# Order of the first transfers and placing of the tail's weights in a decode block with cached attention

## The chip, the cores and the metric

The kernel runs on one core of a Trainium2 chip. The metric is the device time of one execution in microseconds (us). Three runs of the kernel before gave 1055.89, 1056.32 and 1057.12 us, so the median is 1056.32 us. The profile is of one further execution.

## The reference

One token passes through an attention block and a feed-forward block, each scaled and shifted by "modulations" that are computed from a condition vector `c` of 640 numbers:

```python
mod = (silu(c) @ w_mod)                   # 6 vectors of 640: sa, ca, ga, sb, cb, gb
h = layernorm(x) * (1 + ca) + sa          # x: 640 numbers
q = h @ wq                                # 32 heads of 192
o = softmax(q @ k_cache.T * 192**-0.5) @ v_cache     # per head, 8192 cached positions
x = x + ga * (o @ wo)
h = layernorm(x) * (1 + cb) + sb
x = x + gb * (relu(h @ w1 + b1)**2 @ w2 + b2)        # 640 -> 1536 -> 640
```

Everything is in 32-bit floats. The two caches hold 32 heads x 8192 positions x 192 numbers each, which is 6144 KB per head and cache; they make up nearly all of what is read.

## The kernel before

**Tiles.** The positions of a head lie 64 to each of the 128 partitions. There are two buffers for keys, `k_t[0]` and `k_t[1]`, and two for values, `v_t[0]` and `v_t[1]`; head h uses number h mod 2 of each. A transfer of keys also carries, behind the keys, a weight block: with even heads the query weights of the next pair of heads, with odd heads the output weights of an earlier pair (7104 KB in all). Heads 1 and 30 carry none. The names below number the heads from 0 and write k2 for the keys of head 2, v1 for the values of head 1.

**The start.** The first transfer, `wm0`, brings the weights of the first two modulations and the first query weights into `v_t[1]`. Then come k0 in two halves, k1 and v0. While they arrive, the first layernorm and the first query are computed (lines 157 to 206); `m_wm0` (line 207) marks the end of the last reader of `wm0`, after which `v_t[1]` is free for v1.

**A head.** VectorE (DVE in the profile) multiplies the keys by the query in place, in two halves (L288), and sums over each row (L293, L297), with GpSimd (POOL) folding part of it (L291). L301 takes the largest score of a partition, a matmul (L231) brings the partitions together, L306 takes the maximum and ScalarE (ACT) the exponentials (L312). TensorE (PE) multiplies them with the values in 24 matmuls of 512 columns (L225, `pe_values`). With each even head TensorE also computes the query of the next pair out of the weights that lie behind that head's keys in `k_t[0]` (L237, `pe_query`, five matmuls of 384 columns). After a pair, VectorE normalises the two outputs (`dve_project`, L328 to L333), a small matmul turns them (L242), and GpSimd multiplies them with the output weights in `k_t[1]` (L319, L322, `pool_project`).

**The order of the work.** No scheduler sets it: each engine runs its instructions as the code writes them. TensorE's order is that of `pe_pair`: values of the last pair's second head, maximum of the even head, query of the next pair, turn of the last pair, values of the even head, maximum of the odd head, sums. Pairs 1 to 14 run in a hardware loop on TensorE (L267 on); pair 15 is written out behind it, without a query.

**The queue of transfers.** SyncE (SP) issues all transfers from one queue, in the order of the code, and waits there until a buffer is free. In the loop over heads (line 344 on), the transfer of k(h+2) stands first: it waits for the end of VectorE's and GpSimd's work on k(h), with an even h also for the query that is read from the same buffer (`done["q", i + 1]`), with an odd h for the output projection. The transfer of v(h+1) stands behind it and waits for the values matmuls of head h-1, or with head 0 for `m_wm0`.

**The tail.** The last four kinds of transfer bring weights into buffers that have come free: `wm1` (output weights of the last pair and the modulations ga, sb, cb) into `k_t[0]`, `w1` into `v_t[0]`, and `gw2` (the modulation weights of the last gate, gb, and then `w2`) into `k_t[1]` in four pieces, the first with the gate's 1600 KB and the first six of w2's twelve blocks. TensorE computes ga (20 matmuls of 160 columns, L158), the last turn (L427), the attention output (L435), sb and cb in three portions between the steps of the second layernorm (L158 again, 320 columns), `h @ w1` (L461), the gate gb (L158, from the first piece of `gw2`) and the product with w2 (L485, 48 matmuls of 160 columns, waiting for the pieces one by one). VectorE adds and squares between them (L467 to L470) and finishes with L488 and L489.

The semaphore of a transfer is in the last argument of `dma`: `w_sem[1]` for `wm1`, `w_sem[2]` for `w1`, `w_sem[3]` to `w_sem[6]` for the four pieces.

Of the kernel before, what the change touches and what calls it, by code (L numbers as in the profile page):

```python
# [35 lines left out]
SMALL = 2 * KB + FB + KB  # L36
W0 = KB * 2 * D + WQ + SMALL
W1M = WO + KB * 3 * D
GW2 = KB * D + FB * D
W2_CUT = (KB * D + 6 * D, KB * D + 9 * D, KB * D + 11 * D, GW2)  # L40
EPS = 1e-5


# [23 lines left out]
        return self.sem, self.n  # L67


def block_kernel(nc, kw, ky, vc, wm0, wm1, w1, gw2, out):  # L70
# [37 lines left out]
    def dma(dst, src, s):  # L108
        nc.sync.dma_start(dst, src).then_inc(s, 16)
# [3 lines left out]
    def keys_of(h):  # L113
        return kw[WITH_W.index(h)] if h in WITH_W else ky[WITHOUT_W.index(h)]
# [38 lines left out]
    def mod(target, w, n, blocks):  # L153

        for b in blocks:
            wb = w[:, b * n * D:(b + 1) * n * D].rearrange("p (m n) -> p m n", m=n)
            for g in range(G):
                i = pe.matmul(target[32 * g:32 * (g + 1), :n * DG], e_t[:, b:b + 1].to_broadcast([P, 32]),  # L158
                              wb[:, :, DG * g:DG * (g + 1)], start=(b == 0), stop=(b == KB - 1))
        return T.mark(i)  # L160
# [57 lines left out]
    def pe_values(s):  # L218
        T.take(b_sem[s], 16)
        T.take(tk_p[s])  # L220
        t = v_t[s][:, :].rearrange("p (j g n) -> p j g n", g=NV, n=E * ED)
        n = NPOS // E
        for j in range(n):
            for g in range(NV):
                i = pe.matmul(ps_o[s][32 * g:32 * (g + 1), :], p_t[s][:, E * j:E * (j + 1)].rearrange("p e r -> p (e r)"),  # L225
                              t[:, j, g], start=(j == 0), stop=(j == n - 1))
# [42 lines left out]
    for i in range(2, NPAIR - 1):  # L269
        pe_pair(i, False)  # L270
    pe_pair(NPAIR - 1, True)


    landed = {s: [0, 0] for s in range(2)}
# [1 line left out]
    def dve_keys(h, between):  # L276
        s = h % 2
        q = qb[h // 2 % 2][:, DH * (h % 2):DH * (h % 2 + 1)]
        t = k_t[s][:, :HD].rearrange("p (i d) -> p i d", d=DH)
        V.wait(done["qb", h // 2])  # L280
        for c in range(2):
            a, b = c * HALF, (c + 1) * HALF
            if h == 0:
                V.wait((k_sem[0][c], 16))
            else:
                V.wait((k_sem[s][1], 16 * (h // 2 + 1)))
            pr, r = t[:, a:b], sc[s][:, a:b]
            m_mul = V.mark(v.tensor_mul(pr, pr, q[:, None, :].to_broadcast([P, HALF, DH])))  # L288
# [12 lines left out]
        v.tensor_reduce(mp[s][:, :], sc[s][:, :], axis=AX.X, op=ALU.max).then_inc(tk_m, 1)  # L301
# [76 lines left out]
    wm1_t, w1_t, gw_t = k_t[0], v_t[0], k_t[1]  # L378
    dma(wm1_t[:, :W1M], wm1, w_sem[1])
    S.wait(done["v", H - 2])  # L380
    dma(w1_t[:, :KB * FF], w1, w_sem[2])
    S.wait(*done["k", H - 1])
    S.wait(done["wo", NPAIR - 2])
    a = 0
    for n, b in enumerate(W2_CUT):
        dma(gw_t[:, a:b], gw2[:, a:b], w_sem[3 + n])
        a = b

    m_v = T.mark(pe_values(1))
    done["v", H - 1] = m_v  # L390

    tail = [k_t[0][:, W1M:], k_t[1][:, GW2:], v_t[0][:, KB * FF:]]

    def room(which, n):
        r = tail[which][:, :n]
        tail[which] = tail[which][:, n:]
        return r

    mods = room(2, 4 * DG)
    x1, x_t, gb2, y, f, fT, hT = (room(2, n) for n in (DG, DG, DG, DG, FG, FG, DG))  # L400
# [17 lines left out]
    spread(bbt, bbc, FB + KB)  # L418

    T.wait((w_sem[1], 16))  # L420
    w_a, w_b = wm1_t[:, WO:WO + KB * D], wm1_t[:, WO + KB * D:W1M]
    ps_ga, ps_b, ps_g, ps_f, ps_y = ps_q, ps_mx[0], ps_mx[1], ps_o[0], ps_o[1]
# [5 lines left out]
    V.wait(m_ga)  # L428
    v.tensor_copy(mods[:, :DG], ps_ga[:, :DG])
    V.wait(m_turn)  # L430
    T.wait(V.mark(v.tensor_copy(oT[:, :], ps_oT[:, :NV])))
    wo = wm1_t[:, :WO].rearrange("p (j n) -> p j n", j=NV)
    for j in range(NV):
        for g in range(G):
            i = pe.matmul(ps_att[32 * g:32 * (g + 1), :DG], oT[:, j:j + 1].to_broadcast([P, 32]), wo[:, j, DG * g:DG * (g + 1)],  # L435
                          start=False, stop=(j == NV - 1))
    m_att = T.mark(i)
    m_b = mod(ps_b, w_b, 2, range(0, 2))
    V.wait(m_att)
    V.wait(V.mark(v.tensor_mul(x1, ps_att[:, :DG], mods[:, :DG])))  # L440
    m_x1 = V.mark(v.tensor_add(x1, x1, x_t))
    last = {}

    def before():
        mod(ps_b, w_b, 2, range(2, 4))

    def scale_b():
        last["b"] = mod(ps_b, w_b, 2, range(4, 5))
        V.wait(last["b"])
        V.wait(V.mark(v.tensor_copy(mods[:, DG:3 * DG], ps_b[:, :2 * DG])))  # L450
        V.wait(V.mark(v.tensor_scalar(cb1, mods[:, 2 * DG:3 * DG], 1.0, None, op0=ALU.add)))
        return cb1

    m_h2 = layernorm(x1, 32, s2, m2, xm2, sq2, ss2, sd2, rs2, h2, scale_b, mods[:, DG:2 * DG], 16, m_x1, before)
    V.wait(m_h2)
    m_hT = V.mark(v.transpose(hT, h2))
    T.wait(m_hT, (w_sem[2], 16))
    hT3 = hT.rearrange("p (b r) -> p b r", r=32)
    for b in range(KB):
        for g in range(G):  # L460
            i = pe.matmul(ps_f[32 * g:32 * (g + 1), :FG], hT3[:, b], w1_t[:, b * FF + FG * g:b * FF + FG * (g + 1)],  # L461
                          start=(b == 0), stop=(b == KB - 1))
    m_f = T.mark(i)
    T.wait((w_sem[3], 16))
    m_g = mod(ps_g, gw_t[:, :KB * D], 1, range(KB))
    V.wait(m_f)
    V.wait(V.mark(v.tensor_add(f, ps_f[:, :FG], bbt[:, :FG])))  # L467
    V.wait(V.mark(v.tensor_scalar(f, f, 0.0, None, op0=ALU.max)))
# [8 lines left out]
    fT3 = fT.rearrange("p (b r) -> p b r", r=32)  # L477
    for b in range(FB):
        for n, c in enumerate(W2_CUT):
            if KB * D + b * D < c:  # L480
                T.wait((w_sem[3 + n], 16))
                break
        for g in range(G):
            o = KB * D + b * D + DG * g
            i = pe.matmul(ps_y[32 * g:32 * (g + 1), :DG], fT3[:, b], gw_t[:, o:o + DG], start=(b == 0), stop=(b == FB - 1))  # L485
    m_y = T.mark(i)
    V.wait(m_y, m_x2)
    V.wait(V.mark(v.tensor_mul(y, ps_y[:, :DG], gate)))  # L488
# [45 lines left out]
```

## Time and profile before

| | |
|---|---|
| median of 3 runs | 1056.32 us |
| the profiled execution's own time | 1058.37 us |
| its span | 1057.0 us |
| read from HBM | 451.82 MB |
| VectorE busy | 828.7 us (78%) |
| TensorE busy | 400.3 us (38%) |
| GpSimd busy | 315.0 us (30%) |
| mean granted TensorE clock | 0.682 |

The span runs from the first to the last instruction of the record, and 1.37 us of the execution's own time lie outside it. The profiled execution is 2.05 us longer than the median of the runs. The times in the rows below are us from the start of the span. A row of the timeline gives start, duration, engine, line, operation, tiles and count, and in brackets how long the engine was idle and what released it. Each matmul in 32-bit floats shows as two instructions, so x40 stands for 20 matmuls of the code. PEclk is the share of the TensorE clock that was granted; it takes the values 0.50 and 1.00 and means of the two. "SPq" rows are the issuing of transfers, not the transfers.

### The profile page before, as it was taken

Reading aid. Unit: us, or ns where it says so; the run is one execution under the profiler, and the core shown is the slowest. Engines: PE = TensorE matmul, PEld = TensorE weight load, DVE = VectorE, ACT = ScalarE, POOL = GpSimd, SP = SyncE. Lnnn points to the kernel's source line nnn. Section 1 sums busy time; section 2 is a strip of 40 time slices with the busy share of each in tenths; the row PEclk is TensorE's granted clock in tenths of the full one; section 3 lists DMA queues with packets and bytes.
Section 4 is the critical chain, followed back from the end, with each engine's and each line's share of the span. In section 5 each row is a group of like instructions: output and inputs, shape, how many; then the busy total and the mean of one; then the engine's idle time right before and its main releaser. Section 6 shows DMA issues by size and latency. Waiting matters only on the chain.

```text
span 1057.0 us, 5274 instructions
## 1 busy us (share of the span) xinstructions
PE 400.3 (38%) x2160; PEld 142.5 (13%) x2160; DVE 828.7 (78%) x401; ACT 31.3 (3%) x87; POOL 315.0 (30%) x131
## 2 busy tenths in 40 slices
PE   3064314353332435313344431434433244532176
PEld 1021101111010111101111110111101011110023
DVE  1899878788887878878787987878888787988842
ACT  1010000000000000000000000000000000000000
POOL 0222242424215142331515224242421514234140
PEclk8576667666566766657676666767656676666688
DMA  9999999999999999999999999999999999999997
GB/s 398 441 378 439 430 434 438 430 430 441 423 440 434 431 428 441 428 438 436 424 432 437 432 436 434 426 439 430 435 434 434 432 431 432 433 433 436 430 426 302
DMA packets 10388, 451.97 MB, mean 428 GB/s; under 512 B 1156, under 2 KB 1160, under 8 KB 1544
## 3 DMA queue, kind: packets, MB, share of 16 engines
q1 hardware_dynamic: 10376, 451.83, 99.1%
q8 instruction: 6, 0.10, 0.0%
q14 instruction: 6, 0.05, 0.0%
HBM read 451.82 MB, written 0.00 MB: 427 GB/s over the span
## 4 chain that ended last, share of the span: by engine, by line
DMA 50%; DVE 28%; POOL 16%; PE 1%; issue 1%; SPq 0%
DMA k<-in_kw 47%; DVE k L288 20%; POOL acc L322 7%; DVE sc L293 6%; POOL k L319 5%; POOL k L291 4%; DMA k<-in_gw 3%; DVE sc L297 2%; PE ps_o L485 0%; PE ps_mx L158 0%; DVE oT L342 0%; PE ps_mx L231 0%; SPq L55 0%; DVE v L488 0%; DVE v L489 0%
## 5 line engine op out<-in xcount | busy, mean ns | idle before, releaser
L288 DVE TENSOR_TENSOR k<-k,qb 128x6144 f32<-128x6144 f32 x64 | 419.8, 6559 | 145.8 <-DMA k<-in_kw 134.4
L225 PE MATMUL ps_o<-v,p 128*32 128x512 f32 x1536 | 294.5, 740 | 562.0 <-PEq L59 562.0
L291 POOL TENSOR_TENSOR k<-k 128x1344 f32<-128x1344 f32 x64 | 194.6, 3041 | 697.6 <-DVE k L288 697.6
L293 DVE TENSOR_REDUCE sc<-k 128x18 f32<-128x3456 f32 x64 | 240.2, 3753 | 2.2
L225 PEld LDWEIGHTS ps_o<-v,p 128*32 128x32 f32 x1536 | 79.3, 133 | 751.5 <-issue 751.5
L297 DVE TENSOR_REDUCE sc<-k 128x14 f32<-128x1344 f32 x64 | 98.7, 1542 | 0.0
L322 POOL TENSOR_TENSOR acc<-acc,k 128x640 f32<-128x640 f32 x45 | 68.9, 1532 | 3.5
L237 PE MATMUL ps_q<-k,h 128*128 128x384 f32 x150 | 53.5, 506 | 0.0
L319 POOL TENSOR_TENSOR k<-k,oT 128x1920 f32<-128x1920 f32 x15 | 50.8, 3386 | 0.0
L237 PEld LDWEIGHTS ps_q<-k,h 128*128 128x128 f32 x150 | 28.7, 199 | 17.3 <-issue 2.4
L306 DVE TENSOR_REDUCE nm<-ps_mx 128x1 f32<-128x128 f32 x32 | 9.3, 292 | 27.5 <-PE ps_mx L231 27.5
L231 PE MATMUL ps_mx<-ident,mp 128*128 128x128 f32 x64 | 15.8, 329 | 37.3 <-PEq L59 36.9
L312 ACT ACTIVATE p<-sc,nm 128x256 f32<-128x256 f32 x32 | 16.1, 503 | 462.6 <-DVE nm L306 431.7
L331 DVE SCALAR_TENSOR_TENSOR om<-ps_o,r,mask 96x512 f32<-96x512 f32 x32 | 23.9, 747 | 1.1
L214 ACT ACTIVATE qb<-ps_q 128x384 f32<-128x384 f32 x16 | 7.9, 491 | 503.1 <-PE ps_q L237 495.5
L333 DVE TENSOR_REDUCE os<-om 96x64 f32<-96x512 f32 x32 | 21.8, 682 | 1.1
L231 PEld LDWEIGHTS ps_mx<-ident,mp 128*128 128x128 f32 x64 | 9.9, 194 | 64.7 <-issue 64.7
L246 PE MATMUL ps_sum<-sp,ones 128*128 128x2 f32 x32 | 5.9, 253 | 18.7 <-PEq L59 18.7
L158 PE MATMUL ps_o<-v,silu 128*32 128x320 f32 x40 | 4.4, 606 | 14.6 <-DVE silu L151 14.6
L143 DVE COPY small<-v 128x27 f32<-128x27 f32 x1 | 0.2, 179 | 11.7 <-DMA v<-in_wm 11.7
L242 PE MATMUL ps_oT<-quad,os 96*128 96x3 f32 x30 | 5.5, 254 | 8.1 <-PEq L59 8.1
L158 PE MATMUL ps_mx<-k,silu 128*32 128x320 f32 (+1 forms) x80 | 6.2, 455 | 4.8 <-DMA k<-in_gw 4.8
(85 smaller groups left out, 84.8 us busy)
## 6 DMA issues: line engine op xcount, KB each, us to landing
k<-in_kw SPq DMA_DIRECT2D x29, 7104.0 KB, 33.8
v<-in_vc SPq DMA_DIRECT2D x32, 6144.0 KB, 47.7
k<-in_ky SPq DMA_DIRECT2D x2, 6144.0 KB, 37.5
k<-in_wm SPq DMA_DIRECT2D x1, 5760.0 KB, 50.0
v<-in_wm SPq DMA_DIRECT2D x1, 4173.5 KB, 12.7
k<-in_kw SPq DMA_DIRECT2D x1, 4032.0 KB, 28.7
v<-in_w SPq DMA_DIRECT2D x1, 3840.0 KB, 27.2
k<-in_gw SPq DMA_DIRECT2D x1, 3520.0 KB, 30.4
```

The lines of the kernel that those rows point to most:

```text
L225: i = pe.matmul(ps_o[s][32 * g:32 * (g + 1), :], p_t[s][:, E * j:E * (j + 1)].rearrange("p e r -> p (e r)"), t[:, j, g], start=(j == 0), s ...
L231: return pe.matmul(ps_mx[s][:, :P], mp[s][:, :].to_broadcast([P, P]), ident[:, :], start=True, stop=True)
L237: i = pe.matmul(ps_q[:, :PW], h1[:, b:b + 1].to_broadcast([P, P]), w[:, b], start=(b == 0), stop=(b == KB - 1))
L288: m_mul = V.mark(v.tensor_mul(pr, pr, q[:, None, :].to_broadcast([P, HALF, DH])))
L291: m_fold = L.mark(pool.tensor_add(half, half, pr[:, KEEP:, DH // 2:]))
L293: o = v.tensor_reduce(r[:, :KEEP], pr[:, :KEEP], axis=AX.X, op=ALU.add)
L297: m_sc = V.mark(v.tensor_reduce(r[:, KEEP:], half, axis=AX.X, op=ALU.add))
L312: act.activation(p_t[s][:, :, :], sc[s][:, :, None].to_broadcast([P, NPOS, 32 // E]), AF.Exp, bias=nm[s][:, :], accum_out=sp[:, s:s + 1]). ...
L319: m = L.mark(pool.tensor_mul(w, w, oT[:, :, None].to_broadcast([P, NV, D])))
L322: m = L.mark(pool.tensor_add(acc[:, :], acc[:, :], w[:, j]))
L331: V.wait(V.mark(v.scalar_tensor_tensor(om[:n], ps_o[a][:n].rearrange("p (d e) -> p d e", e=E), r2[:n, a:a + 1], mask[:n, None, :].to_broad ...
L333: o = v.tensor_reduce(os_[:n, a], om[:n], axis=AX.X, op=ALU.add)
```

## The change

**Head.** With head 0, v1 is issued ahead of k2 instead of behind it. The order of all later transfers of keys and values is the same.

**Tail weights.** The gate's weights (1600 KB) move from the front of the last group to the end of the transfer of `w1`: `w1g` has 5440 KB, and the first piece of `w2` has 1920 KB where the first piece of `gw2` had 3520 KB. In what order the bytes come stays the same. TensorE now waits for `w1g` as a whole, computes the gate (from `v_t[0]`) and then `h @ w1`. The three other modulations ga, sb and cb are one group of 20 matmuls of 480 columns, ahead of the last turn; the portions between the steps of the layernorm are gone, and VectorE copies the group (L431 of the new code) while TensorE computes the attention output.

**Loop.** The values of a pair's second head stand at the end of `pe_pair` instead of at the beginning of the next. Pair 15 is in the loop, so it computes a query as well (five matmuls whose result nobody uses), and the transfer of `wm1`, which overwrites what they read, waits for them.

On SyncE's queue, right behind the first transfers (names as above; the number of a buffer stands behind its name), before:

```order
L109 DMA v0<-in_vc 128x12288
L109 DMA k0<-in_kw 128x14208 [waits pe,pool,dve]
L109 DMA v1<-in_vc 128x12288
L109 DMA k1<-in_kw 128x14208 [waits pool,dve]
L109 DMA v0<-in_vc 128x12288 [waits pe]
```

and after the change:

```order
L109 DMA v0<-in_vc 128x12288
L109 DMA v1<-in_vc 128x12288 [waits dve,pe]
L109 DMA k0<-in_kw 128x14208 [waits pe,pool,dve]
L109 DMA k1<-in_kw 128x14208 [waits pool,dve]
L109 DMA v0<-in_vc 128x12288 [waits pe]
```

The second and third of these rows have changed places: the values of head 1 (into `v1`) no longer stand behind the wait of the keys of head 2 (into `k0`).

On TensorE, at the end of the program, from the last matmuls of the attention output to the first of w2 (w1, w2 and w3 in brackets are the semaphores of the transfers), before:

```order
L435 MATMUL ps_att<-k,oT 32x160 x11
L158 MATMUL ps_mx<-k,silu 32x320 x8
L163 MATMUL ps_sum<-k,ones 128x1 [waits dve]
L461 MATMUL ps_o<-v 32x384 [waits w2,dve]
L461 MATMUL ps_o<-v 32x384 x19
L158 MATMUL ps_mx<-k,silu 32x160 [waits w3]
L158 MATMUL ps_mx<-k,silu 32x160 x19
L485 MATMUL ps_o<-k,v 32x160 [waits dve]
L485 MATMUL ps_o<-k,v 32x160 x23
```

and after, from the group of three modulations on:

```order
L158 MATMUL ps_mx<-k,silu 32x480 [waits w1]
L158 MATMUL ps_mx<-k,silu 32x480 x19
L427 MATMUL ps_oT<-quad,os 128x3 [waits tk_o]
L436 MATMUL ps_att<-k,oT 32x160 [waits dve]
L436 MATMUL ps_att<-k,oT 32x160 x11
L163 MATMUL ps_sum<-k,ones 128x1 [waits dve] x2
L158 MATMUL ps_mx<-v,silu 32x160 [waits w2]
L158 MATMUL ps_mx<-v,silu 32x160 x19
L451 MATMUL ps_o<-v 32x384 [waits dve]
L451 MATMUL ps_o<-v 32x384 x19
L473 MATMUL ps_o<-k 32x160 [waits w3,dve]
L473 MATMUL ps_o<-k 32x160 x23
```

The gate's 20 matmuls stood behind those of w1 and waited for the first piece of the last group; now they stand ahead of them and wait for the transfer that also brings w1.

The diff, cut to its core:

```diff
-W2_CUT = (KB * D + 6 * D, KB * D + 9 * D, KB * D + 11 * D, GW2)
+W1G = KB * FF + KB * D
+W2_CUT = (6 * D, 9 * D, 11 * D, FB * D)
...
         steps = []
-        if i:
-            steps.append((("v", 2 * i - 1), lambda: pe_values(1)))
         steps.append((("mx", 2 * i), lambda: pe_max(0)))
-        if i + 1 < NPAIR:
-            steps.append((("q", i + 1), pe_query))
+        steps.append((("q", i + 1), pe_query))
         if i:
             steps.append((("oT", i - 1), pe_turn))
-        steps += [(("v", 2 * i), lambda: pe_values(0)), (("mx", 2 * i + 1), lambda: pe_max(1)), (("sum", i), pe_sum)]
+        steps += [(("v", 2 * i), lambda: pe_values(0)), (("mx", 2 * i + 1), lambda: pe_max(1)), (("sum", i), pe_sum),
+                  (("v", 2 * i + 1), lambda: pe_values(1))]
...
-    with nc.Fori(1, NPAIR - 1, engines=bass.OrderedEngineSet([ET.PE]), head_slot={ET.PE: 0}):
+    with nc.Fori(1, NPAIR, engines=bass.OrderedEngineSet([ET.PE]), head_slot={ET.PE: 0}):
...
-            if c and s == 0 and h + 2 < H:
+            if c and s == 0:
                 o.then_inc(tk_q, 1)
...
-        if h + 2 < H:
+        def load_keys():
             S.wait(*done["k", h])
...
+        def load_values():
+            S.wait(*(m_wm0 if h == 0 else (done["v", h - 1],)))
+            dma(v_t[1 - s][:, :], vc[h + 1], b_sem[1 - s])
+
         if h == 0:
-            S.wait(*m_wm0)
-        elif h + 1 < H:
-            S.wait(done["v", h - 1])
-        if h + 1 < H:
-            dma(v_t[1 - s][:, :], vc[h + 1], b_sem[1 - s])
+            load_values()
+        if h + 2 < H:
+            load_keys()
+        if 0 < h < H - 1:
+            load_values()
...
     S.wait(*done["k", H - 2])
+    S.wait(done["q", NPAIR])
...
-    dma(w1_t[:, :KB * FF], w1, w_sem[2])
+    dma(w1_t[:, :W1G], w1g, w_sem[2])
...
-    m_ga = mod(ps_ga, w_a, 1, range(KB))
+    m_b = mod(ps_b, wm1_t[:, WO:], 3, range(KB))
...
-    T.wait(m_hT, (w_sem[2], 16))
+    T.wait((w_sem[2], 16))
+    m_g = mod(ps_g, w1_t[:, KB * FF:], 1, range(KB))
+    T.wait(m_hT)
...
-    T.wait((w_sem[3], 16))
-    m_g = mod(ps_g, gw_t[:, :KB * D], 1, range(KB))
```

Beside this the small buffers of the tail lie in other places of the same large buffers, and `wm1`'s modulation weights are laid out as one group of three.

More of the change, by code (lines that the diff above doesn't have):

```diff
@@ L38 @@
 W1M = WO + KB * 3 * D
-GW2 = KB * D + FB * D
-W2_CUT = (KB * D + 6 * D, KB * D + 9 * D, KB * D + 11 * D, GW2)
+W1G = KB * FF + KB * D
+W2_CUT = (6 * D, 9 * D, 11 * D, FB * D)
 EPS = 1e-5
@@ L67, in last, with block_kernel @@
         return self.sem, self.n
-def block_kernel(nc, kw, ky, vc, wm0, wm1, w1, gw2, out):
+def block_kernel(nc, kw, ky, vc, wm0, wm1, w1g, w2, out):
     sem = nc.alloc_semaphore
@@ L266, in block_kernel @@
     pe_pair(0, True)
-    with nc.Fori(1, NPAIR - 1, engines=bass.OrderedEngineSet([ET.PE]), head_slot={ET.PE: 0}):
+    with nc.Fori(1, NPAIR, engines=bass.OrderedEngineSet([ET.PE]), head_slot={ET.PE: 0}):
         pe_pair(1, True)
-    for i in range(2, NPAIR - 1):
+    for i in range(2, NPAIR):
         pe_pair(i, False)
-    pe_pair(NPAIR - 1, True)
     landed = {s: [0, 0] for s in range(2)}
@@ L368, in block_kernel @@
             dma(k_t[s][:, :w], keys_of(h + 2), k_sem[s][1])
+        def load_values():
+            S.wait(*(m_wm0 if h == 0 else (done["v", h - 1],)))
+            dma(v_t[1 - s][:, :], vc[h + 1], b_sem[1 - s])
         if h == 0:
-            S.wait(*m_wm0)
-        elif h + 1 < H:
-            S.wait(done["v", h - 1])
-        if h + 1 < H:
-            dma(v_t[1 - s][:, :], vc[h + 1], b_sem[1 - s])
+            load_values()
[3 more added lines that the diff above has]
+            load_values()
     S.wait(*done["k", H - 2])
-    wm1_t, w1_t, gw_t = k_t[0], v_t[0], k_t[1]
+    S.wait(done["q", NPAIR])
+    wm1_t, w1_t, w2_t = k_t[0], v_t[0], k_t[1]
     dma(wm1_t[:, :W1M], wm1, w_sem[1])
     S.wait(done["v", H - 2])
-    dma(w1_t[:, :KB * FF], w1, w_sem[2])
+    dma(w1_t[:, :W1G], w1g, w_sem[2])
     S.wait(*done["k", H - 1])
@@ L385, in block_kernel @@
     for n, b in enumerate(W2_CUT):
-        dma(gw_t[:, a:b], gw2[:, a:b], w_sem[3 + n])
+        dma(w2_t[:, a:b], w2[:, a:b], w_sem[3 + n])
         a = b
-    m_v = T.mark(pe_values(1))
-    done["v", H - 1] = m_v
-    tail = [k_t[0][:, W1M:], k_t[1][:, GW2:], v_t[0][:, KB * FF:]]
+    tail = [k_t[0][:, W1M:], k_t[1][:, FB * D:], v_t[0][:, W1G:]]
     def room(which, n):
@@ L397, in room @@
         return r
-    mods = room(2, 4 * DG)
-    x1, x_t, gb2, y, f, fT, hT = (room(2, n) for n in (DG, DG, DG, DG, FG, FG, DG))
+    mods = room(1, 4 * DG)
+    x1, x_t, gb2, y, hT = (room(2, DG) for _ in range(5))
+    f, fT = room(1, FG), room(1, FG)
     cb1, xm2, sq2, h2 = (room(1, DG) for _ in range(4))
@@ L420, in block_kernel @@
     T.wait((w_sem[1], 16))
-    w_a, w_b = wm1_t[:, WO:WO + KB * D], wm1_t[:, WO + KB * D:W1M]
-    ps_ga, ps_b, ps_g, ps_f, ps_y = ps_q, ps_mx[0], ps_mx[1], ps_o[0], ps_o[1]
-    m_ga = mod(ps_ga, w_a, 1, range(KB))
+    ps_b, ps_g, ps_f, ps_y = ps_mx[0], ps_mx[1], ps_o[0], ps_o[1]
+    m_b = mod(ps_b, wm1_t[:, WO:], 3, range(KB))
     dve_project(NPAIR - 1)
@@ L427, in block_kernel @@
     m_turn = T.mark(pe.matmul(ps_oT[:, :NV], os_[:96].rearrange("p a d -> p (a d)"), quad[:96, :], start=True, stop=True))
-    V.wait(m_ga)
-    v.tensor_copy(mods[:, :DG], ps_ga[:, :DG])
     V.wait(m_turn)
     T.wait(V.mark(v.tensor_copy(oT[:, :], ps_oT[:, :NV])))
+    V.wait(m_b)
+    v.tensor_copy(mods[:, :3 * DG], ps_b[:, :3 * DG])
+    cb1_of = V.mark(v.tensor_scalar(cb1, ps_b[:, 2 * DG:3 * DG], 1.0, None, op0=ALU.add))
     wo = wm1_t[:, :WO].rearrange("p (j n) -> p j n", j=NV)
@@ L437, in block_kernel @@
     m_att = T.mark(i)
-    m_b = mod(ps_b, w_b, 2, range(0, 2))
-    V.wait(m_att)
+    V.wait(m_att, cb1_of)
     V.wait(V.mark(v.tensor_mul(x1, ps_att[:, :DG], mods[:, :DG])))
     m_x1 = V.mark(v.tensor_add(x1, x1, x_t))
[L442 to L454, printed above, removed]
+    m_h2 = layernorm(x1, 32, s2, m2, xm2, sq2, ss2, sd2, rs2, h2, lambda: cb1, mods[:, DG:2 * DG], 16, m_x1, lambda: None)
     V.wait(m_h2)
     m_hT = V.mark(v.transpose(hT, h2))
-    T.wait(m_hT, (w_sem[2], 16))
+    T.wait((w_sem[2], 16))
+    m_g = mod(ps_g, w1_t[:, KB * FF:], 1, range(KB))
+    T.wait(m_hT)
     hT3 = hT.rearrange("p (b r) -> p b r", r=32)
@@ L479, in block_kernel @@
         for n, c in enumerate(W2_CUT):
-            if KB * D + b * D < c:
+            if b * D < c:
                 T.wait((w_sem[3 + n], 16))
@@ L483, in block_kernel @@
         for g in range(G):
-            o = KB * D + b * D + DG * g
-            i = pe.matmul(ps_y[32 * g:32 * (g + 1), :DG], fT3[:, b], gw_t[:, o:o + DG], start=(b == 0), stop=(b == FB - 1))
+            o = b * D + DG * g
+            i = pe.matmul(ps_y[32 * g:32 * (g + 1), :DG], fT3[:, b], w2_t[:, o:o + DG], start=(b == 0), stop=(b == FB - 1))
     m_y = T.mark(i)
@@ L523 @@
                                column(B_b1, FB), column(B_b2, KB)], axis=1),
-        "wm1": np.concatenate([wo[-1], rows(wm[:, 2 * D:3 * D], KB), rows(wm[:, 3 * D:5 * D], KB)], axis=1),
-        "w1": rows(B_w1, KB),
-        "gw2": np.concatenate([rows(wm[:, 5 * D:], KB), rows(B_w2, FB)], axis=1),
+        "wm1": np.concatenate([wo[-1], rows(wm[:, 2 * D:5 * D], KB)], axis=1),
+        "w1g": np.concatenate([rows(B_w1, KB), rows(wm[:, 5 * D:], KB)], axis=1),
+        "w2": rows(B_w2, FB),
     }
```

## Prediction

> **What bounds the kernel now.** I began with the page, at the transfers: the busy share of the transfer engines in 40 slices, and the total.
>
> ```profile
> DMA  9999999999999999999999999999999999999997
> GB/s 398 441 378 439 430 434 438 430 430 441 423 440 434 431 428 441 428 438 436 424 432 437 432 436 434 426 439 430 435 434 434 432 431 432 433 433 436 430 426 302
> ...
> q1 hardware_dynamic: 10376, 451.83, 99.1%
> ```
>
> The stream of bytes sets the time, and the change moves no byte more or less. Only the third slice (52.9 to 79.3 us, 378 GB/s) and the last (from 1030.6, 302 GB/s) can give anything. The window in the first dip (its last two figures are the busy share of the transfers and GB/s, the one ahead of them the granted clock):
>
> ```profile
> 58.00:60.00 2.00, 1.36 (x4) 0.44 (x2) 2.00 (x1) 0.58 (x2) 0.00 (x0) 0.85 0.00 0
> ```
>
> From 58 to 60 us nothing moves at all. The timeline says why, and shows the next heads:
>
> ```profile
> 21.84 6.48 PE L205 MATMUL ps_q<-v,h 128*128 128x384 f32 x10 [1.43 <-DVE h L182]
> ...
> 52.43 0.22 DVE L301 TENSOR_REDUCE mp<-sc 128x1 f32<-128x64 f32 x1
> ...
> 53.36 6.00 PE L237 MATMUL ps_q<-k,h 128*128 128x384 f32 x10
> ...
> 59.47 0.33 SPq L109 DMA_DIRECT2D k<-in_kw  x1
> ...
> 79.97 6.56 DVE L288 TENSOR_TENSOR k<-k,qb 128x6144 f32<-128x6144 f32 x1 [1.16 <-DMA k<-in_kw]
> ...
> 94.70 9.47 PE L225 MATMUL ps_o<-v,p 128*32 128x512 f32 x48 [14.49 <-PEq L59]
> ...
> 103.53 0.22 DVE L301 TENSOR_REDUCE mp<-sc 128x1 f32<-128x64 f32 x1
> ...
> 104.42 3.39 PE L237 MATMUL ps_q<-k,h 128*128 128x384 f32 x10
> ...
> 107.90 0.33 SPq L109 DMA_DIRECT2D k<-in_kw  x1
> ...
> 111.22 6.56 DVE L288 TENSOR_TENSOR k<-k,qb 128x6144 f32<-128x6144 f32 x1 [3.23 <-DMA k<-in_kw]
> ...
> 140.96 0.33 SPq L109 DMA_DIRECT2D k<-in_kw  x1
> ...
> 142.62 6.56 DVE L288 TENSOR_TENSOR k<-k,qb 128x6144 f32<-128x6144 f32 x1 [6.62 <-DMA k<-in_kw]
> ```
>
> From the chain of waits one row more, of head 5:
>
> ```profile
> 173.87 6.57 DVE k L288
> ```
>
> The keys k2 go out at 59.47, right behind the query in their buffer, when the queue has run dry, and v1 behind them. They are usable at 79.97, k3 at 111.22, k4 at 142.62, k5 at 173.87.
>
> **Head: the pause goes.** The keys' transfers have this size:
>
> ```profile
> k<-in_kw SPq DMA_DIRECT2D x29, 7104.0 KB, 33.8
> ```
>
> From 111.22 to 173.87 the stream carries two transfers of 7104 KB and two of 6144 KB in 62.65 us, so 16.8 us for keys and 14.5 us for values. k2 took 79.97 - 59.47 = 20.5 us from its issue, so a start on an empty queue costs 20.5 - 16.8 = 3.7 us of stream. `m_wm0`, the end of L205, is over at 28.3, so in the new order v1 joins the queue while k1 and v0 still flow, and the 3.7 us go.
>
> **Head: and part comes back at k4.** The next rows move. Without the pause v1 lands at 94.5 - 3.7 - 16.8 = 74.0, where 94.5 is k2's 79.97 plus 14.5 (94.70 confirms it); k2 lands at 90.8, which is 10.8 us later than now, k3 at 107.6, v2 at 122.1. VectorE therefore starts head 2 at 90.8, and its maximum stands at 90.8 + (103.53 - 79.97) = 114.4. k4 must wait for that and for the query behind it. Now this takes 107.90 - 103.53 = 4.4 us, with TensorE warm from the values of head 1 (94.70 + 9.47 = 104.17). In the new order those values have landed at 74.0, run as soon as head 1's exponentials are there, about 80 us, and end near 89.5; TensorE then does nothing for 25 us. How the clock stands after such a gap:
>
> ```profile
> 42.00:52.00 10.00, 0.00 (x0) 0.00 (x0) 9.97 (x3) 0.00 (x0) 3.03 (x1) 0.50 0.99 428
> ...
> 80.00:94.00 14.00, 0.22 (x2) 0.13 (x1) 13.97 (x4) 0.00 (x0) 3.03 (x1) 0.50 0.98 424
> ...
> 100.00:114.00 14.00, 8.17 (x44) 3.38 (x38) 9.72 (x10) 0.98 (x3) 1.38 (x1) 0.97 0.98 426
> ```
>
> At 0.50 head 0's query took 6.00 us and 59.47 - 52.43 = 7.0 us from the maximum to the issue. So k4 goes out between 118.8 (warm) and 121.4 (cold throughout); I take 120.6, nearer to the cold row, with the clock rising within the query. To follow v2 (122.1) without a gap it would have to go out 3.7 us ahead, at 118.4. So a second pause of 2.2 us (0.4 to 3.0) takes the place of the first, and the head gains 3.7 - 2.2 = **1.5 us** (0.7 to 3.3). There it ends: VectorE starts head 3 at about 118.9 (114.4 and some 4.5 us for the maximum and the outputs of the first pair), k5 goes out 140.96 - 111.22 = 29.7 us later, near 148.6, and v3 ends behind k4 near 155.6, so that 3.7 us ahead of it there are 3 us to spare.
>
> **Tail before.** The steps there, from the timeline:
>
> ```profile
> 1011.85 0.33 SPq L109 DMA_DIRECT2D v<-in_w  x1
> ...
> 1029.95 1.56 PE L158 MATMUL ps_q<-k,silu 128*32 128x160 f32 x40 [3.78 <-DMA k<-in_wm]
> ...
> 1032.09 1.02 PE L435 MATMUL ps_att<-k,oT 128*32 128x160 f32 x24 [0.25 <-DVE oT L431]
> ...
> 1036.22 0.26 ACT L177 ACTIVATE k<-ps_sum,eps_t 128x1 f32<-128x1 f32 x1 [21.68 <-PE ps_sum L163]
> ...
> 1037.72 0.16 DVE L180 RECIPROCAL k<-k 128x1 f32<-128x1 f32 x1
> ...
> 1038.70 0.34 DVE L456 STREAM_TRANSPOSE v<-k 128x160 f32<-128x160 f32 x1
> ...
> 1039.20 3.43 PE L461 MATMUL ps_o<-v 128*32 128x384 f32 x40 [2.35 <-DMA v<-in_w]
> ...
> 1042.69 0.56 DVE L467 TENSOR_TENSOR v<-ps_o,k 128x384 f32<-128x384 f32 x1 [3.64 <-PE ps_o L461]
> ...
> 1044.27 0.58 DVE L470 STREAM_TRANSPOSE v<-v 128x384 f32<-128x384 f32 x1
> ...
> 1047.43 2.89 PE L158 MATMUL ps_mx<-k,silu 128*32 128x160 f32 x40 [4.80 <-DMA k<-in_gw]
> ```
>
> The end of the chain of waits:
>
> ```profile
> 1016.97 30.42 DMA k<-in_gw
> ...
> 1050.32 4.15 PE ps_o L485 x96
> ```
>
> The transfers, with KB and us from issue to landing:
>
> ```profile
> v<-in_w SPq DMA_DIRECT2D x1, 3840.0 KB, 27.2
> k<-in_gw SPq DMA_DIRECT2D x1, 3520.0 KB, 30.4
> ...
> k<-in_gw SPq DMA_DIRECT2D x1, 320.0 KB, 33.8
> ```
>
> And the clock in the windows of the tail:
>
> ```profile
> 1021.00:1045.00 24.00, 15.17 (x194) 6.79 (x187) 9.25 (x24) 0.26 (x1) 0.00 (x0) 1.00 0.98 420
> 1045.00:1052.00 7.00, 4.57 (x72) 3.41 (x76) 0.98 (x3) 0.00 (x0) 0.00 (x0) 0.51 0.66 268
> 1052.00:1055.00 3.00, 2.42 (x72) 1.86 (x64) 0.47 (x2) 0.00 (x0) 0.00 (x0) 1.00 0.00 0
> ```
>
> The first piece of the last group lands at 1047.39; gate (L158) and w2 (L485) follow and end at 1054.47. w1 landed at 1011.85 + 27.2 = 1039.05, the last 320 KB at about 1018.3 + 33.8 = 1052.1 (the four issues lie within 1.75 us). At full clock 20 matmuls of 160 columns take 1.56 us, at 0.51 they take 2.89. From 1047.43 to about 1051.9 the clock was half, which cost 4.5 / 2 = 2.2 us; so the 48 matmuls of L485 are worth 7.04 - 2.2 - 1.56 = 3.3 us at full clock.
>
> **Tail: the gate leaves the end, and w1 gets late.** What is taken away behind 1047.39 is the gate, 1.6 to 2.9 us. But `h @ w1` now waits for `w1g`. Between w1 and the first piece 3520 KB took 1047.39 - 1039.05 = 8.3 us, so the gate's 1600 KB take 3.8 us, and `w1g` lands at 1042.85, less the head's 1.5: 1041.35. From there the work is in series:
> - the gate, cold, since TensorE has had only two small sums since about 1035: 2.9 us, to 1044.25;
> - L451 (as L461, 20 matmuls of 384): 3.4 us warm, 6.9 cold. If the half clock lasts 4.5 us again, 1.6 us of it fall here: 4.2 us (3.4 to 5.1), to 1048.45;
> - VectorE's four steps, 1042.69 to 1044.85, with the waits at both ends 2.3 us: 1050.75;
> - all 48 matmuls of w2: 3.3 us, or 5.0 if the clock drops in this pause of 2.3 us; I take 3.65, to **1054.4**.
>
> The last piece (1052.1 - 1.5, then four matmuls) is over at 1051 and no longer last. So in this execution's terms the tail eats the head's gain: 1054.4 against 1054.47 (1053.2 to 1056.6), and an own time of 1058.37 - 0.1 = 1058.3.
>
> The three modulations in one group hide. They take 3 x 1.56 = 4.7 us from 1028.45, so the attention output starts at 1033.15 plus the 0.65 that the turn takes now (1031.45 to 1032.09), at 1033.8; from there to the end of L456 it is now 1039.04 - 1032.09 = 6.95 us, of which about 1.2 us go, VectorE's wait for sb and cb (from 1036.48, when L177 ends, to L180 at 1037.72). So the layernorm ends near 1039.6, or 2 us later cold, ahead of the gate's end at 1044.25. The useless query of pair 15 and `wm1`'s wait for it hide too: they delay its issue by 4 to 6 us, and `wm1` sits in the queue for 50 us as the row shows:
>
> ```profile
> k<-in_wm SPq DMA_DIRECT2D x1, 5760.0 KB, 50.0
> ```
>
> Queued behind it on SyncE are w1g and w2, whose own waits end later. The loop's branch now follows the second head's values, where VectorE has 3.23 us to spare: nothing.
>
> **Against the median.** The profiled execution is 2.05 us above the median of the runs (1058.37 to 1056.32), and the half clock at its end cost 2.2 us. If the runs mostly miss that stretch (with L461 a little later, TensorE would not have idled the 4.80 us), the new median stands at the new own time, 1058.3, for there the gap before the gate, 6 us, is always long enough. If recording costs the 2.05 us, it is 1056.3. The sizes agree, so I weigh the first two to one: 1056.3 + 2/3 x 2.0 = **1057.6**.
>
> [...]
>
> **Rivals.** *The idle time goes and stays away* (0.11). TensorE would have to be warm at 114.7, then k4 goes out at 118.8 and the head keeps 3.3 us. The chain of the tail ends at 1052.6, 1.9 below now: 1056.5 own time, 1054.4 as median by the constant offset, down to 1053.6 with a short half clock in L451. Against it: 25 us of idle TensorE, where every such window shows 0.50.
>
> *The serial chain at half clock* (0.32), slower. Half clock lasts 6 us from the gate's start (L451 5.0 us) and returns in VectorE's 2.3 us (w2 5.0 us), and the head keeps 0.7: 1042.15 + 2.9 + 5.0 + 2.3 + 5.0 = 1057.35, own time 1061.2, median up to 1059.2 by the constant offset. By the first reading it decides as soon as the chain ends after 1054.5, at 1058.4. For it: four serial steps on one late transfer.
>
> *The change does nothing to the time* (inside my forecast): the second pause is as long as the first and the tail's gain and loss cancel, 1056.3.
>
> **How the numbers follow.** A difference of 0.2%, 2.1 us, is about what can be told from no change: 1054.2 to 1058.4. My forecast, a moved pause and a moved wait, lies inside with 0.57; faster 0.11, slower 0.32. The range is 1054.2 (head at 2.6, L451 and w2 at their short ends: a chain to 1052.15, the constant offset) to 1059.6 (head at 0.7, L451 at 5.0, the first reading: a chain to 1055.65).
>
> **What would show it.** Right: no pause at 58 us but one near 121 to 123, a cold L237 of 5 to 6 us in front of it, k4's keys usable 0.7 to 3.3 us ahead of 142.62; in the tail the gate released by `w1g` near 1041 and w2's 48 matmuls released by VectorE, not by a transfer. Wrong: no second pause, or w2 waiting for its pieces.

## The result and the profile after

The changed kernel takes 1061.30 us (median of 6 runs, 1060.77 to 1062.09), the kernel before 1056.33 us (6 runs, 1055.89 to 1057.12). The ratio is 1.0047, with a 95% interval of 1.0034 to 1.0060: slower by 5.0 us, and outside the range of the prediction. The profiled execution has a span of 1060.0 us and an own time of 1061.31 us, in the middle of its runs.

The transfers in 40 slices of the span, from the page of the changed kernel:

```profile
GB/s 396 443 441 415 401 388 424 445 425 446 428 426 440 427 438 438 437 416 443 429 436 429 439 426 435 436 430 430 445 431 422 441 422 441 430 436 435 433 429 284
...
q1 hardware_dynamic: 10376, 451.83, 98.8%
```

The dip has moved from the third slice to the fourth, fifth and sixth (79.5 to 159 us), and it has grown. In windows (the last two columns are the busy share of the transfers and GB/s, the one ahead of them the granted clock):

```profile
58.00:60.00 2.00, 0.00 (x0) 0.00 (x0) 1.97 (x2) 1.91 (x4) 0.65 (x1) 1.00 1.08 467
...
120.00:122.00 2.00, 2.00 (x6) 1.20 (x5) 2.00 (x2) 0.00 (x0) 0.00 (x0) 0.79 0.17 74
...
154.00:156.00 2.00, 0.00 (x0) 0.00 (x0) 2.00 (x1) 0.00 (x0) 1.92 (x2) 0.50 0.12 49
```

The pause at 58 is gone. One near 121 has come, as forecast, and one near 155 that was not forecast; below they are the first, the second and the third pause. The timeline at these places (the first row is two issues, k2 at 57.59 and k3 some 19 us later):

```profile
57.59 19.00 SPq L109 DMA_DIRECT2D k<-in_kw  x2
...
92.33 6.56 DVE L285 TENSOR_TENSOR k<-k,qb 128x6144 f32<-128x6144 f32 x1 [14.60 <-DMA k<-in_kw]
...
116.80 5.39 PE L237 MATMUL ps_q<-k,h 128*128 128x384 f32 x10
...
120.33 6.54 DVE L285 TENSOR_TENSOR k<-k,qb 128x6144 f32<-128x6144 f32 x1
...
122.28 0.33 SPq L109 DMA_DIRECT2D k<-in_kw  x1
...
145.31 7.81 DVE L285 TENSOR_TENSOR k<-k,qb 128x6144 f32<-128x6144 f32 x1
...
156.22 0.33 SPq L109 DMA_DIRECT2D k<-in_kw  x1
```

and GpSimd alone ahead of that last issue:

```profile
145.18 10.95 POOL L319 TENSOR_TENSOR acc<-acc,k 128x640 f32<-128x640 f32 x3
```

k5 (156.22) waits for the three adds of the first output projection. They took 10.95 us. All 45 adds of the run, with the shortest, the middle and the longest one in ns:

```profile
L319 POOL TENSOR_TENSOR acc<-acc,k x45: 1528/1530/7730, 145.2 to 1017.2; 128x640 f32<-128x640 f32 x45
```

In the kernel before, the same line reads:

```profile
L322 POOL TENSOR_TENSOR acc<-acc,k x45: 1531/1531/1535, 136.1 to 1015.4; 128x640 f32<-128x640 f32 x45
```

So one add of 45 took 7.73 us where every one had taken 1.53. It ran beside VectorE's product of head 4 (145.31), which took 7.81 us and not 6.55. The first two of the three adds by themselves, and a window in which GpSimd goes from one to the other (the figure ahead of the clock is GpSimd's busy time, with two instructions in it):

```profile
145.18 9.34 POOL L319 TENSOR_TENSOR acc<-acc,k 128x640 f32<-128x640 f32 x2
...
146.50:148.00 1.50, 0.29 (x2) 0.21 (x1) 1.50 (x1) 0.00 (x0) 1.42 (x2) 0.50 0.76 328
```

So the first add took its 1.53 us, and the second is the long one. It ended at 154.52, 1.40 us after the product (145.31 + 7.81 = 153.12), nearly the 1.53 us that an add of the kernel before takes.

The end, from the chain of waits of the changed kernel:

```profile
1013.14 31.46 DMA v<-in_w1g
...
1044.65 2.89 PE ps_mx L158 x40
1047.55 4.19 PE ps_o L451 x40
...
1051.76 0.57 DVE k L455
...
1053.34 0.59 DVE k L458
...
1053.97 3.51 PE ps_o L473 x96
```

The chain starts at the landing of `w1g` and holds the gate, w1, VectorE and w2 in series. The clock in that stretch:

```profile
1045.00:1048.00 3.00, 3.00 (x48) 1.93 (x44) 0.00 (x0) 0.00 (x0) 0.00 (x0) 0.50 0.98 415
1048.00:1052.00 4.00, 3.69 (x40) 1.09 (x32) 0.24 (x1) 0.00 (x0) 0.00 (x0) 0.84 0.93 376
```

And the first piece of w2, for the place of the stream: issued at 1018.78, it took 30.4 us.

```profile
k<-in_w SPq DMA_DIRECT2D x1, 1920.0 KB, 30.4
```

It landed at 1049.2, where the same bytes had landed at 1047.39: the stream is 1.8 us later, not 1.5 earlier.

### The profile page after: what moved, and what is told of

It is laid out like the page before. It is cut to its first block, busy times and chain, and to the rows that moved or that the text cites. A ratio compares the mean times of both kernels' runs of the same rounds, so it can differ in the third digit from the quotient of the medians.

```text
span 1060.0 us, 5217 instructions
## 1 busy us (share of the span) xinstructions
PE 405.2 (38%) x2130; PEld 144.9 (14%) x2130; DVE 829.4 (78%) x400; ACT 31.3 (3%) x87; POOL 321.0 (30%) x131
## 5 line engine op out<-in xcount | busy, mean ns | idle before, releaser
L225 PE MATMUL ps_o<-v,p 128*32 128x512 f32 x1536 | 291.4, 733 | 514.3 <-PEq L59 514.3
L290 DVE TENSOR_REDUCE sc<-k 128x18 f32<-128x3456 f32 x64 | 240.2, 3753 | 2.2
L319 POOL TENSOR_TENSOR acc<-acc,k 128x640 f32<-128x640 f32 x45 | 75.1, 1668 | 3.5
L237 PE MATMUL ps_q<-k,h 128*128 128x384 f32 x160 | 60.8, 532 | 0.0
L237 PEld LDWEIGHTS ps_q<-k,h 128*128 128x128 f32 x160 | 32.6, 213 | 20.3 <-issue 6.0
L246 PEld LDWEIGHTS ps_sum<-sp,ones 128*128 128x128 f32 x32 | 5.2, 203 | 21.5 <-issue 21.5
L298 DVE TENSOR_REDUCE mp<-sc 128x1 f32<-128x64 f32 x32 | 7.0, 220 | 1.1
```

Of the source, the lines that this page charges most:

```text
L237: i = pe.matmul(ps_q[:, :PW], h1[:, b:b + 1].to_broadcast([P, P]), w[:, b], start=(b == 0), stop=(b == KB - 1))
L319: m = L.mark(pool.tensor_add(acc[:, :], acc[:, :], w[:, j]))
```

## The experiments

All ratios are to runs of the kernel before on the same chip (29 to 35 of them), with 95% intervals; each experiment has 7 to 12 runs.

### The four parts alone

**a_head**: only the order at the head.

```diff
-        if h + 2 < H:
+        def load_keys():
...
+        def load_values():
+            S.wait(*(m_wm0 if h == 0 else (done["v", h - 1],)))
+            dma(v_t[1 - s][:, :], vc[h + 1], b_sem[1 - s])
+
         if h == 0:
-            S.wait(*m_wm0)
-        elif h + 1 < H:
-            S.wait(done["v", h - 1])
-        if h + 1 < H:
-            dma(v_t[1 - s][:, :], vc[h + 1], b_sem[1 - s])
+            load_values()
+        if h + 2 < H:
+            load_keys()
+        if 0 < h < H - 1:
+            load_values()
```

> Only the order at the head is changed: v1 is issued ahead of k2, the tail and the loop are those of before. Theory (stream): the head's order alone makes the stream of bytes 1.8 us later, by two new pauses (k4 issued at 122.3, k5 at 156.2) that cost more than the old one; so 1058.1 us, against 1056.3 before. Rival (tail): the head's gains and losses cancel over runs, and all 5.0 us come from the tail; 1056.3 us or a little less.

1.0023 (1.0014 to 1.0032). The head's order alone costs about 2.4 us: the first theory holds, and the loss is somewhat larger than the 1.8 us that it said.

**a_gate_w1**: only the gate's weights behind w1.

```diff
-    T.wait(m_hT, (w_sem[2], 16))
+    T.wait((w_sem[2], 16))
+    m_g = mod(ps_g, w1_t[:, KB * FF:], 1, range(KB))
+    T.wait(m_hT)
...
-    T.wait((w_sem[3], 16))
-    m_g = mod(ps_g, gw_t[:, :KB * D], 1, range(KB))
```

> Only the gate's weights ride with w1 and the gate stands ahead of w1's matmuls; ga, sb and cb stay in their portions, head and loop are those of before. Theory: the wait for w1g puts gate, w1, VectorE's steps and w2 in series behind a transfer 3.8 us later; 3.2 us of the 5.0 come from here, so 1059.5 us. Rival (group): the tail's loss comes from the group of three modulations that delays the attention output, and this part alone costs nothing; 1056.3 us.

1.0018 (1.0009 to 1.0027), 1.9 us: of the theory's sign, but less than its 3.2. The timeline of its slowest run (1060.52) shows the series, with w1's matmuls partly cold (4.90 us, 3.43 in the kernel before):

```profile
1043.21 2.89 PE L158 MATMUL ps_mx<-v,silu 128*32 128x160 f32 x40 [5.99 <-DMA v<-in_w1g]
1045.88 4.90 PE L464 MATMUL ps_o<-v 128*32 128x384 f32 x40
...
1053.07 3.47 PE L486 MATMUL ps_o<-k 128*32 128x160 f32 x96 [2.29 <-DVE k L471]
```

**a_loop**: only the last pair in the loop, and the values of a pair's second head at its end.

```diff
-    with nc.Fori(1, NPAIR - 1, ...
+    with nc.Fori(1, NPAIR, ...
...
+    S.wait(done["q", NPAIR])
```

> Only the last pair goes into the loop, with its useless query and the wait of wm1 for it, and the values of a pair's second head close the pair. Theory: hidden, 1056.3 us. Rival: the loop's branch behind the values and the wait delay the keys or wm1; 1057 us or more.

0.9999 (0.9990 to 1.0008): no difference shown.

**a_mods**: only the three modulations in one group.

```diff
-    m_ga = mod(ps_ga, w_a, 1, range(KB))
+    m_b = mod(ps_b, wm1_t[:, WO:W1M], 3, range(KB))
```

> Only ga, sb and cb are one group of 480 columns ahead of the last turn; gate and w1 stay as before. Theory: hidden behind the wait for the first piece of the last group, 1056.3 us (within 0.7 either way, since the clock at the end may stand otherwise). Rival (group): the attention output is 5 to 6 us later, the layernorm ends after w1 and gate would want it, 1058 us or more.

1.0001 (0.9992 to 1.0010): hidden, though the group took more than the forecast's 4.7 us and w1's matmuls started 2.4 us later than before:

```profile
1029.50 5.93 PE L158 MATMUL ps_mx<-k,silu 128*32 128x480 f32 x40 [4.03 <-DMA k<-in_wm]
...
1041.61 6.35 PE L448 MATMUL ps_o<-v 128*32 128x384 f32 x40 [1.71 <-DVE v L443]
```

The four add up to 1.0041, against 1.0047 (1.0034 to 1.0060) for the change: no difference shown.

### What the head pays for

**b_pool_first**: a_head, and VectorE waits with head 4 until GpSimd has ended the projection.

```diff
         V.wait(done["qb", h // 2])
+        if h == 4:
+            V.wait(done["wo", 0])
```

> As a_head (v1 ahead of k2, all else as before), with one wait more: VectorE starts the products of head 4 only when GpSimd has ended the first output projection. Theory (shared work of VectorE and GpSimd): in a_head GpSimd's adds of the projection stretch from 4.75 to 10.9 us because VectorE's product runs beside them, and k5, which waits for them, goes out at about 155; with the wait they take 4.75 us, k5 goes out near 150, the third pause is gone and the stream is 1.6 us earlier than before at k5, not 1.3 later: 2.7 to 3 us below a_head, 0.9985 of before. Rival: GpSimd is slow there for another reason (the transfers into the same buffers) or k6 is late in its place; time as a_head, 1.002 of before.

The place in the timeline (first GpSimd, then the issue of k5 and VectorE):

```profile
144.61 4.75 POOL L324 TENSOR_TENSOR acc<-acc,k 128x640 f32<-128x640 f32 x3
149.44 0.33 SPq L109 DMA_DIRECT2D k<-in_kw  x1
149.44 6.56 DVE L290 TENSOR_TENSOR k<-k,qb 128x6144 f32<-128x6144 f32 x1 [4.62 <-POOL acc L324]
```

With nothing beside them the adds take 4.75 us again, k5 goes out at 149.44, and the third pause is gone (426 GB/s from 154 to 156). So the stretch of the adds is shown to come from VectorE's product, and the third pause from the stretch. On the stream the pause was worth 3.1 us: the keys of head 7 are used from 234.74 here and from 237.84 in a_head.

The stretch itself is only put off. It comes back with the next projection, beside the product of head 6, where the code has no such wait:

```profile
202.31 10.95 POOL L324 TENSOR_TENSOR acc<-acc,k 128x640 f32<-128x640 f32 x3
...
203.49 6.76 DVE L290 TENSOR_TENSOR k<-k,qb 128x6144 f32<-128x6144 f32 x1 [0.97 <-DMA k<-in_kw]
...
213.34 0.33 SPq L109 DMA_DIRECT2D k<-in_kw  x1
```

k7 goes out at 213.34, where the kernel before had issued it at 203.62, and yet no pause follows: the stream moves 410 GB/s from 210 to 216. There the queue still had bytes ahead of k7; at 155 it had run dry (49 GB/s in the changed kernel). So of these two late issues the one at a dry queue made a pause, and the one at 410 GB/s made none.

The time is 1.0003 (0.9994 to 1.0012), about 2 us below a_head and not the 2.7 to 3 that were expected, so the gain against before is not there. In the profiled execution (1055.49, where the runs lie between 1055.47 and 1058.46) the stream does have it: the keys of the last head are used from 985.29, in the kernel before from 987.25. Where the runs lose these 2 us is not shown.

**c_no_pauses**: the same, and k4 in two transfers, its keys not waiting for the cold query.

```diff
+            if h == 2:
+                dma(k_t[0][:, :HD], keys_of(4)[:, :HD], k_sem[0][0])
             if s == 0:
                 S.wait(done["q", i + 1])
...
-            dma(k_t[s][:, :w], keys_of(h + 2), k_sem[s][1])
+            a = HD if h == 2 else 0
+            dma(k_t[s][:, a:w], keys_of(h + 2)[:, a:], k_sem[s][1])
```

> As b_pool_first (v1 ahead of k2, VectorE waits for GpSimd before head 4), and k4 is two transfers, the keys without waiting for the query of the pair behind them. Theory: the second pause (1.7 us in b_pool_first) was the cold query's, so it goes as well and none is left; k4 lands near 139.7, k5 near 171.0, as in b_split, and the time is that of b_split, 0.9984 of before. Rival: what holds k4 back is VectorE, which got k2 late, not the query; the pause stays, 1.000 of before.

0.9986 (0.9977 to 0.9995). The keys of head 4 go out at 115.38, ahead of the query (116.31), and at both places the stream flows:

```profile
120.00:122.00 2.00, 1.29 (x6) 0.76 (x4) 2.00 (x1) 0.80 (x3) 0.00 (x0) 1.00 1.03 442
...
154.00:156.00 2.00, 1.16 (x6) 0.44 (x9) 2.00 (x1) 0.00 (x0) 0.00 (x0) 0.50 0.98 426
```

The second pause was the query's. With both causes taken away the new order is a gain, so it is these two waits that make it a loss. On the stream the second weighs little: the keys of head 7 are used from 234.50 here and from 234.74 in b_pool_first, those of the last head from 984.69 and 985.29. The time fell by more, about 1.8 us; the two intervals leave 0.4 to 3 us, and what else fell was not followed.

**b_split**: the old order, k2 in two transfers.

```diff
+            if h == 0:
+                dma(k_t[0][:, :HD], keys_of(2)[:, :HD], k_sem[0][0])
             if s == 0:
                 S.wait(done["q", i + 1])
...
+            a = HD if h == 0 else 0
+            dma(k_t[s][:, a:w], keys_of(h + 2)[:, a:], k_sem[s][1])
```

> The kernel before with one edit: k2 is two transfers, the keys as soon as head 0's keys have been used, and the query weights behind them once the query has been read; v1 stays behind. Theory: the keys go out at 52.5 instead of 59.5, more than 3.7 us ahead of the end of v0, so the first pause goes; VectorE gets k2 at about 77, not later than now, so no later pause takes its place, and the stream keeps 3.5 us: 0.9967 of before, 1053.5. Rival: the pause comes back in another place as in the change (gain below 1 us).

0.9984 (0.9974 to 0.9994), 1.6 us and not 3.5. The keys went out at 52.03, the pause is gone (442 GB/s from 58 to 60), and VectorE got k3 at 108.49 instead of 111.22:

```profile
108.49 6.56 DVE L290 TENSOR_TENSOR k<-k,qb 128x6144 f32<-128x6144 f32 x1 [2.39 <-DMA k<-in_kw]
```

So the first pause was worth 2.7 us in the profiled execution, not the 3.7 that issue-to-landing less stream time had given. Over the runs it was worth less again; how long the first query ran cold in each of them was not followed.

### What the tail pays for

**b_gate_own**: a_gate_w1, but the gate's weights as a transfer of their own, and w1's matmuls first.

```diff
-    dma(w1_t[:, :W1G], w1g, w_sem[2])
+    dma(w1_t[:, :KB * FF], w1g[:, :KB * FF], w_sem[2])
+    dma(w1_t[:, KB * FF:W1G], w1g[:, KB * FF:], w_sem[8])
...
-    T.wait((w_sem[2], 16))
-    m_g = mod(ps_g, w1_t[:, KB * FF:], 1, range(KB))
-    T.wait(m_hT)
+    T.wait(m_hT, (w_sem[2], 16))
...
     m_f = T.mark(i)
+    T.wait((w_sem[8], 16))
+    m_g = mod(ps_g, w1_t[:, KB * FF:W1G], 1, range(KB))
```

> As a_gate_w1 (gate's weights behind w1), but as a transfer of its own with its own semaphore, and w1's matmuls first, the gate behind them. The bytes come in the same order. Theory: w1's matmuls start at 1039 as before, the gate at 1043 in TensorE's gap, w2 follows its pieces and the end hangs on the last piece at 1052.1; 0.999 of before (the runs of before with a half clock at the end lose up to 2.5 us against it), 2.5 to 3 us below a_gate_w1. Rival: a gate ahead of w2 costs the same wherever its bytes land, and the time stays at 1.002 of before.

0.9991 (0.9982 to 1.0000), as expected, though the interval just reaches the time of before. Now w1 and gate lie in one warm stretch (granted clock 1.00 from 1038 to 1052), and the end hangs on the pieces of w2:

```profile
1041.08 3.43 PE L463 MATMUL ps_o<-v 128*32 128x384 f32 x40 [2.25 <-DVE v L458]
1044.33 1.54 PE L158 MATMUL ps_mx<-v,silu 128*32 128x160 f32 x40
...
1050.48 1.27 PE L487 MATMUL ps_o<-k 128*32 128x160 f32 x24 [0.50 <-DMA k<-in_w]
```

**c_gate_behind**: a_gate_w1 with one transfer, but the gate's matmuls behind those of w1.

```diff
-    T.wait((w_sem[2], 16))
-    m_g = mod(ps_g, w1_t[:, KB * FF:], 1, range(KB))
-    T.wait(m_hT)
+    T.wait(m_hT, (w_sem[2], 16))
...
     m_f = T.mark(i)
+    m_g = mod(ps_g, w1_t[:, KB * FF:], 1, range(KB))
```

> As a_gate_w1, one transfer w1g, but TensorE does w1's matmuls first and the gate behind them. This tells the late landing from the place of the gate. Theory: the series behind the landing loses the gate's 2.9 us, w1's matmuls run cold in its place (6 us instead of 4.9), so 1.5 to 2 us less than a_gate_w1: 1.000 to 1.0005 of before. Rival: the landing alone is the cost, the time is that of a_gate_w1, 1.0018.

1.0000 (0.9990 to 1.0010). Against the kernel before the late landing costs nothing that shows; the gate in front of w1 does; whether by its 2.9 us alone or also by the clock that w1 then meets, was not followed run by run. Against b_gate_own it may cost up to about 1 us, which the intervals do not tell apart. The cold w1 of the theory was not there: in this profiled execution w1's matmuls took 3.47 us (3.43 in the kernel before), and the end hung on the last piece again:

```profile
1010.93 31.20 DMA v<-in_w1g
...
1042.26 3.47 PE ps_o L462 x40
...
1051.42 0.52 PE ps_o L485 x8
```

**c_no_head**: the changed kernel with the old order at the head.

```diff
-        if h == 0:
-            load_values()
         if h + 2 < H:
             load_keys()
-        if 0 < h < H - 1:
+        if h < H - 1:
             load_values()
```

> The changed kernel with the old order at the head (k2 ahead of v1); loop and tail are changed. Theory: stream as before, so 1.0018 to 1.0024 of before (the tail's share, as a_gate_w1), about 3 us below the changed kernel's 1.0047. Rival: the head's order matters only together with the tail, and the time stays near 1.004.

1.0016 (1.0007 to 1.0025), as a_gate_w1.

**c_after_gate_own**: the changed kernel with the repair of b_gate_own in its tail (the same edit).

> The changed kernel with one repair in the tail: the gate's weights are a transfer of their own behind w1, and TensorE does w1's matmuls first. Theory: only the head's loss is left, 1.0015 to 1.0023 of before, as a_head. Rival: the group of three modulations, harmless alone, shows once the gate is out of the way; 1.003 or more.

1.0022 (1.0013 to 1.0031), as a_head. Head and tail stand beside each other, and each can be taken back alone.

### A version that beats both

**b_best**: b_split and b_gate_own together, in the kernel before (both edits as above).

> b_split and b_gate_own together. Theory: the gains add, 3.5 us from the stream and about 1 us from the end: 0.9957 of before, 1052.5. Rival: one of the two gives nothing beside the other, 0.9967 or 0.999.

0.9971 (0.9960 to 0.9983): median 1053.90 us, six of seven runs between 1053.86 and 1054.03 and one at 1054.91. The gain is 3.0 us against the expected 4.5, since b_split gave less. The profiled execution is the one at 1054.91; its w1 was partly cold (4.80 us from 1040.51), and behind it the clock stays up:

```profile
1045.00:1052.00 7.00, 5.13 (x140) 4.10 (x132) 3.56 (x9) 0.00 (x0) 0.00 (x0) 1.00 0.31 122
```

## Why the prediction was wrong

**The first pause goes**: right, at 467 GB/s from 58 to 60. Its size was not: 3.7 us forecast, 2.7 in b_split. Issue to landing less stream time counts too much; why, no run here shows. k2 came at 92.33, not 90.8.

**The second pause at k4**: right in place and cause. L237 ran 5.39 us cold (3.39 at this place in the kernel before), k4 went out at 122.28 (forecast 120.6, late by k2's 1.5), and c_no_pauses shows that it was the query. Of its size, 2.2 us forecast, the changed kernel shows only the dip to 74 GB/s.

**"There it ends", k5 out near 148.6 with 3 us to spare**: this is the step that failed. The 29.7 us from the start of head 3 to the issue of k5 were read where VectorE stood idle beside GpSimd's adds, waiting for k4. In the new order k4 has landed and VectorE goes on at once with head 4. One add beside VectorE's product then takes 6.2 us more (7.73 for 1.53). k5 went out 156.22 - 120.33 = 35.9 us after the start of head 3, and the third pause (3.1 us by a_head and b_pool_first) took all that was won and more: the stream ends 1.8 us later than in the profiled execution of before, where 1.5 earlier was forecast. The prediction put this stretch of GpSimd's at nothing. b_pool_first shows the cause. I had looked at what each engine waits for, and not at what it runs beside.

In the trace the first add and the product lay beside each other from 145.31 to 146.71 (145.18 + 1.53), and the product took 7.81 us for 6.55; the second add ran beside the rest of the product and took 7.73 us for 1.53. Why the two slow each other, no run here shows.

What is left of the first add when the product starts is about what the product grows by: 1.40 us left and 1.26 more in the changed kernel, 0.35 left and 0.21 more at 203.49 in b_pool_first. And VectorE's sum over a row behind it (L290, from 153.16) ran beside the third add at its usual 3.75 us (all 64 of the run took 3.75).

**The tail's series**: right in its order and in the profiled execution term by term. From the landing of `w1g` forecast and measured are 2.9 and 2.89 for the gate, 4.2 and 4.19 for w1, 2.3 and 2.2 for VectorE, 3.65 and 3.51 for w2. That w1 hit to a hundredth is luck, for it rests on where the clock rises: in the other profiled executions it took 3.43 to 6.35 us. The series hung on the landing, and that came at 1044.61 and not at 1041.35: 3.3 us, of which 1.5 the head did not win and 1.8 it lost.

**Group, query of pair 15, loop**: right that they hide. The group took 5.93 us where 4.7 was forecast, at granted clocks of 0.85 and 0.80 in the windows around it.

**Against the median**: the second reading, the 2.05 us as a constant offset of recording, fell. The profiled execution of the changed kernel is 0.01 us from its median, so recording costs no 2 us. The first reading, to which I had given two thirds, holds in part. The profiled execution of before lay at the slow end of its runs (those beside the experiments lie between 1054.27 and 1058.80), and the gate at its end, 2.89 us cold, took 1.53 to 1.56 in b_split, b_pool_first and c_no_pauses, which have the same tail (and 2.63 and 2.89 in a_loop and a_head). That 6 us of idle TensorE are long enough for the half clock, the traces bear out: behind the first matmuls, each idle stretch of 6.6 us and more ended at 0.50 (32 in the kernel before, 33 in the changed one), and a_gate_w1's gate, behind 5.99 us, took 2.89. But by the first reading the tail alone would cost 3.5 us (1058.3 + 1.5 - 1056.3), and a_gate_w1 and c_no_head measured 1.9 and 1.7.

In own times the sum closes: 1058.3, with the 3.3 us of the stream and 0.2 us less in the tail, gives 1061.4, where 1061.3 was measured. The head is the term that failed: it cost 2.4 us over the runs (a_head), where it was to win 1.5.

The slower rival had its sign from the tail alone (the half clock) and its price from there; what made the change slow was the tail as forecast on top of a head that lost. That the head could lose was in none of the cases. The rival's own time of 1061.2 lies beside the 1061.3 by chance: it starts from 1042.15 with 5.0 us each for w1 and w2, and measured were 1044.61, 4.19 and 3.51.

## What to carry to other kernels

When a transfer is put ahead of another on a queue, what is put back comes late (here k2, usable at 92.33 us for 79.97), and the engine that waits for it then runs at another time beside other engines: follow the new order until the old distances are back, and look for what runs side by side there that did not before. A duration that was read where a neighbour stood idle need not hold beside a busy one: the three adds took 4.75 us and 10.95 us. Ask what still lies ahead of a late transfer on the queue: one late issue left 49 GB/s, another 410. On a path that starts with a late transfer, put the work that others wait for first, and give each transfer its own semaphore (1.0018 in a_gate_w1, 0.9991 in b_gate_own).

## What the runs showed of the hardware

- One add on GpSimd of 128x640 took 7.73 us beside a product on VectorE of 128x6144, and 1.53 us with VectorE idle; the product took 7.81 us there and 6.55 in the median of the 64 products, and the add ended 1.40 us behind it. The stretch of three adds with the long one (10.95 us for 4.75) stands once in the profiled execution of the changed kernel, in that of a_head, and in b_pool_first one projection later; in the kernel before all 45 adds took 1.53.
- Beside the experiments, runs of one kernel on one chip scattered over 2 to 4.4 us (before: 1054.39 to 1058.80 on one of three chips), while b_best, whose keys at the head do not wait for a cold query and whose end does not wait for a cold gate, kept six of seven runs within 0.2 us. What makes the scatter was not followed run by run.
